# Fourier mixing and low-rank mixer: prologue reordered around the arrival of x, filter mirrors cut in pieces, group 0 in fixed order, two batches' steps moved and every reload brought forward in the main loop

## The chip, the cores and the metric

The kernel runs on one core of one Trainium2 chip. The metric is device time in microseconds (us). All runs used here are fast. Each kernel has one profiled run; its span is a little shorter than the run's time (596.6 us of span in a run of 598.55 us). Differences of parts are taken from spans and times of day inside a trace, differences between kernels from ratios. A ratio is the mean time of one kernel's fast runs over that of the kernel before in the same rounds, so it is not quite the ratio of the medians quoted beside it.

The engines in the profile are PE (TensorE matmuls), PEld (its weight loads), DVE (VectorE), ACT (ScalarE), POOL (GpSimd) and SP, which issues DMAs. "Half clock" means that the clock records of a trace show TensorE granted 0.5 of its full clock. A "hole" is a time in which PE stands still.

## The reference

```python
# x (8, 3136, 256), filt_r and filt_i (1569, 256)
X = np.fft.rfft(x, axis=1)
y = np.fft.irfft(X * (filt_r + 1j*filt_i), n=3136, axis=1)
# U (3136, 32), V (32, 3136), w_ch1 (256, 1024), w_ch2 (1024, 256)
h = y.transpose(0, 2, 1) @ U @ V
u = y + h.transpose(0, 2, 1)
out = u + np.maximum(u @ w_ch1, 0) @ w_ch2
```

The Fourier transform of length 3136 = 64 x 49 is done as matmuls with constant matrices: stage 1 over 64 points, a turn, stage 2 over 49 points (z), the product with the filter, and the same way back.

## The kernel before

Batch 0 is worked off alone in a prologue, because nothing else is ready. After it a main loop of 49 groups of 8 steps does the two large matmuls of all batches (`phh` = u @ w1, `pc` = h @ w2), and the transforms of batches 1 to 7 are dealt out over the steps as generators. Engines called `te, ve, se, ge, sy` keep the program's order. Instructions on `nc.tensor` and so on may be moved by the scheduler. In the profile the pinned instructions all have one line, L98, the line of the helper.

Names that return in the views, in the order of the work: `pf` is a result of stage 1 in PSUM (the memory that matmuls write to) and `xh` (for U, `eball`) its copy. `pa` is the turn and `at` its copy; "the first turn" is the first `pa`. `pz` is a result of stage 2 and `uv` its product with the filter. `po` is the first step of the way back and `uh` its copy. U's own steps make `aur`, `ga`, `gb` and `aus`, and the matmuls `ph` use them for the low-rank part.

The prologue's loads and its stage 1, cut:

```python
for c in range(3): load_x(u0, c)                       # POOL's queue
for c in range(3): sy.dma_start(wf[:, ...c...], ...)   # constants of stage 1
sy.dma_start(ulf, ...)                                 # U's last rows
sy.dma_start(mats, mats_d)                             # 366 KB
sy.dma_start(wf[0:64, 3072:3136], ...)                 # 8 KB, for the last rows
...
ve.tensor_copy(ul, ulf)
stage1(... un ..., xhu, 32)             # U, stage 1
stage1_last(32, ul, xhu)                # needs the small wf
fill(4, ...)                            # matmuls on junk, to keep PE's clock
aur = u_turn()
se.copy(fab[0:NR, :, 31, :], st31[0:NR])
mirror(2, 0, ge)
for c in range(3):                      # x of batch 0 in three chunks
    for dh in range(2):
        stage1(... u0.x[c] ..., xh[dh], 128)
    if c == 0: gab = u_z(aur)           # ga on ACT, gb on DVE
    if c == 1: u_rows(aur); ph0 = ...   # aus
    if c: fill(4, ...)
... stage1_last for x
mirror(0, 0, ve); turn1(0); mirror(0, 1, ve); turn1(1)
for i in range(16):                     # pairs of frequencies
    ... turn1(i + 2)
    if i == 3: mirror(1, 0, ve); mirror(1, 1, se)    # 12 slots each
    if i == 9: mirror(2, 1, se)                      # 12 slots
    uvs0[i] = z_product(u0, 2*i, at[i], te, ve)      # pz, then uv on DVE
    ... i1_turned(i - 2)                # po, then uh on ACT
    ... h_part at i = 7, 11, 13
```

`mirror` copies the filter `fab` from partitions 0..63 to 64..127.

The main loop's plan, cut. `f1` is stage 1 of a batch and writes its result to DRAM (`ct`). `mid` reads it back in the other order (`a2`, shown as `a<-ct`) and does z and the way back (`pe`). `ranks` is the low-rank part.

```python
def mid(u):
    for c in range(2): a2[c] = load_a2(u, c)
    for k in range(0, NK, 2): ... z_product ...; yield
...
if u.n == 1:
    deal(f1s[1], 7, 2, 9);    deal(mids[1], 17, 13, 37); rank = (38, 40)
elif u.n == 2:
    deal(f1s[2], 7, 26, 38);  deal(mids[2], 17, 43, 75); rank = (s-20, s-18); x_step[14] = u
else:
    deal(f1s[u.n], 7, s-78, s-66); deal(mids[u.n], 17, s-56, s-23)
    rank = (s-20, s-18); x_step[s-92] = u          # s = 48 * u.n
```

## Time and profile before

| | before |
|---|---|
| time, median of 3 runs | 597.58 us (597.38 to 598.76) |
| stage 1 of x starts / first turn | 21.6 / 35.1 us |
| the 16 filter products (uv) | 36.9 to 62.4 us, 25.5 us |
| last uh copy to first phh | 63.6 to 69.2 us |
| main loop, from the first phh | 527.3 us |

The page of the kernel before: PE's busy time, and the span in 40 slices of 14.9 us with busy tenths, the granted clock in tenths, and DMA's busy tenths.

```profile
PE 554.9 (93%) x4803; PEld 397.3 (67%) x4803; DVE 348.3 (58%) x375; ACT 354.2 (59%) x608; POOL 45.6 (8%) x83
...
PE   5678894999999999999999999999999999999996
...
PEclk9588996999999999999999999999999999999998
DMA  9991048335965479365856568546945642432112
```

PE is full from slice 8 to the last. Slices 1 to 5 (prologue) and slice 7 are not, and in slices 2 and 7 the clock is also low. The sum of 93% hides this: most of the time that can be seen to be lost lies in the first 105 us.

The waits of PE before, over the whole span: total in us, times, longest.

```profile
PE pz L325 <- DMA a<-ct: 12.1, 6, 7.9
PE pf L98 <- DMA wf<-wf: 7.8, 2, 6.4
PE po L98 <- ACT uh L98: 5.6, 3, 2.9
PE pur L98 <- DVE gb L98: 1.9, 1, 1.9
...
PE ph L98 <- ACT aus L98: 1.1, 1, 1.1
```

The first line is the main loop; the other four are the prologue. PE in the prologue before, in order of time (start, duration, what, how many, idle time before and what ended it):

```profile
9.73 0.61 PE L98 MATMUL pf<-wf,un 128*32 128x128 f16 x8 [1.39 <-DMA wf<-wf]
16.77 0.21 PE L98 MATMUL pf<-wf,ul 64*32 64x64 f16 x1 [6.44 <-DMA wf<-wf]
16.91 1.89 PE L98 MATMUL fill<-un,junk 128*128 128x512 f16 x4
18.86 2.76 PE L98 MATMUL ptu<-mats,eball 32*98 32x32 f16 x32
21.55 1.89 PE L98 MATMUL pf<-wf,x 128*128 128x128 f16 x16
```

A single small matmul on U's last rows holds PE until 16.8 us, because its 8 KB of constants stand in SP's queue behind 366 KB: by the DMA records the packets of `mats` run from 7.7 to 13.7 us, those of the small wf from 11.2 to 15.3. The trace's semaphores show x's chunks landed at 10.2, 13.2 and 16.9 us, while their stage 1 begins only at 21.6.

The chain of waits before around batch 1's reload (start, duration, what):

```profile
85.04 4.50 DMA ct<-al
...
89.61 10.98 DMA a<-ct
...
100.63 0.58 PE pz L325
```

PE runs out of earlier work at 92.7 us and stands still for 7.9 us.

### The profile page before, as it was taken

The page shows a single profiled execution, that of the slowest core. Times are in us where ns is not written, and L with a number is a line of the kernel's source. Part 1 is how long each engine was busy: PE and PEld are TensorE (multiplying, and loading weights), DVE is VectorE, ACT ScalarE, POOL GpSimd, SP SyncE. Part 2 cuts the span into 40 slices and gives each one's busy share as a digit, 9 for nine tenths or more (in the row PEclk, how much of TensorE's full clock was granted, in tenths as well). Part 3 has the DMA queues.
Part 4 walks back from the last instruction along what each step waited for, and adds up shares of the span by engine and source line. Part 5 has one row for each costly group of instructions (what it writes and reads, how often), then busy time and mean ns, then how long its engine had stood idle before and what let it go on. Part 6 is the DMA issues. An engine that isn't in the chain of part 4 may idle for free.

```text
span 596.6 us, 11873 instructions
## 1 busy us (share of the span) xinstructions
PE 554.9 (93%) x4803; PEld 397.3 (67%) x4803; DVE 348.3 (58%) x375; ACT 354.2 (59%) x608; POOL 45.6 (8%) x83
## 2 busy tenths in 40 slices
PE   5678894999999999999999999999999999999996
PEld 2445572667767767776777667776777677777775
DVE  4366651896586476656674476547665566433331
ACT  1367662476667556665666566665666566666562
POOL 6650010000100001000100010000100000000000
PEclk9588996999999999999999999999999999999998
DMA  9991048335965479365856568546945642432112
GB/s 203 138 168 27 2 129 203 127 113 180 229 198 151 151 211 205 133 188 174 180 170 192 176 156 197 167 150 187 202 139 181 169 145 75 141 107 89 55 52 106
DMA packets 68610, 88.97 MB, mean 149 GB/s; under 512 B 5644, under 2 KB 52734, under 8 KB 68556
## 3 DMA queue, kind: packets, MB, share of 16 engines
q1 hardware_dynamic: 61516, 72.41, 38.7%
q0 software_dynamic: 7040, 15.82, 16.3%
q8 instruction: 37, 0.61, 0.4%
q14 instruction: 17, 0.14, 0.1%
HBM read 55.85 MB, written 48.17 MB: 174 GB/s over the span
## 4 chain that ended last, share of the span: by engine, by line
PE 78%; DMA 9%; ACT 7%; DVE 3%; issue 2%; SPq 1%; ACTq 0%
PE pc L625 25%; PE phh L602 24%; PE pe L450 7%; DMA a<-ct 6%; PE pz L325 5%; PE pc L630 3%; PE pu L585 3%; PE pf L419 2%; ACT asb L422 2%; DMA wf<-wf 2%; ACT e L461 1%; ACT h L604 1%; PE ph L554 1%; PE po L98 1%; ACT fab L98 1%
## 5 line engine op out<-in xcount | busy, mean ns | idle before, releaser
L604 ACT ACTIVATE h<-phh 128x512 f16<-128x512 f32 x392 | 233.6, 598 | 126.8 <-PE phh L602 125.6
L625 PE MATMUL pc<-w2sb,h 128*128 128x256 f16 x1568 | 241.1, 273 | 0.1
L602 PE MATMUL phh<-ut,w1sb 128*128 128x512 f16 x784 | 239.5, 382 | 0.6 <-DVE ut L594 0.3
L625 PEld LDWEIGHTS <-h 128*128 128x128 f16 x1568 | 150.4, 98 | 77.3 <-issue 2.5
L336 DVE TENSOR_TENSOR uv<-pz,fab 113x1024 f16<-113x1024 f32 x112 | 135.4, 1219 | 36.8 <-PE pz L325 35.9
L636 DVE COPY och<-pc 128x512 f32<-128x512 f32 x98 | 67.6, 690 | 123.2 <-PE pc L630 122.2
L602 PEld LDWEIGHTS <-w1sb 128*128 128x128 f16 x784 | 96.4, 145 | 18.3 <-issue 3.3
L461 ACT CAST e<-pe 98x512 f16<-98x512 f32 x112 | 65.0, 587 | 52.0 <-PE pe L450 51.6
L594 DVE CAST ut<-pu 128x1024 f16<-128x1024 f32 x48 | 58.7, 1222 | 21.2 <-PE pu L585 21.2
L450 PE MATMUL pe<-uv,mats 113*98 113x512 f16 x210 | 62.5, 378 | 0.0
L630 PE MATMUL pc<-mats,ut 128*128 128x128 f16 x392 | 54.1, 220 | 0.0
L325 PE MATMUL pz<-a,mats 98*128 98x512 f16 x105 | 39.5, 385 | 13.0 <-DMA a<-ct 12.1
L630 PEld LDWEIGHTS <-ut 128*128 128x128 f16 x392 | 38.4, 98 | 6.2 <-issue 0.2
L585 PEld LDWEIGHTS <-eball 96*128 96x128 f16 x768 | 29.1, 98 | 9.9 <-issue 1.9
L450 PEld LDWEIGHTS <-mats 113*98 113x98 f16 x210 | 25.4, 124 | 12.6 <-issue 2.8
L488 DVE COPY eball<-h 32x2048 f16<-32x2048 f16 x34 | 22.1, 680 | 19.7 <-ACT h L515 18.4
L425 DVE CAST asb<-pf 128x1024 f16<-128x1024 f32 x21 | 25.6, 1221 | 13.2 <-PE pf L419 13.1
L585 PE MATMUL pu<-sv,eball 96*128 96x64 f16 x768 | 30.6, 193 | 0.5
L160 POOL COPY x<-h 1x1 f16<-1x1 f16 x18 | 2.5, 178 | 363.6 <-ACT h L604 363.6
L419 PE MATMUL pf<-x,wf 128*128 128x256 f16 x168 | 26.1, 273 | 0.6
L98 DVE TENSOR_TENSOR uv<-pz,fab 113x1024 f16<-113x1024 f32 x16 | 19.0, 1221 | 5.8 <-PE pz L98 4.0
L422 ACT CAST asb<-pf 128x1024 f16<-128x1024 f32 x21 | 21.3, 1015 | 1.1 <-PE pf L419 1.0
(88 smaller groups left out, 282.6 us busy)
## 6 DMA issues: line engine op xcount, KB each, us to landing
out_dram<-och SPq DMA_DIRECT2D x48, 512.0 KB
x<-in_x_dram POOLq DMA_DIRECT2D x24, 512.0 KB, 8.5
a<-ct SPq DMA_DIRECT2D x28, 392.0 KB
ct<-e SPq DMA_DIRECT2D x56, 196.0 KB
ct<-asb SPq DMA_DIRECT2D x21, 512.0 KB
eball<-ct SPq DMA_DIRECT2D x84, 128.0 KB
wf<-wf SPq DMA_DIRECT2D x3, 256.0 KB
w1sb<-in_moe_w_ch_dram POOLq DMA_DIRECT2D x1, 512.0 KB, 5.3
```

The source lines that it names most:

```text
L325: te.matmul(pz, wz[0], a2, start=True, stop=True)
L336: ve.tensor_mul(uv.rearrange("p f k d -> p f (k d)"), zin, fin)
L419: nc.tensor.matmul(pf[:, j], wf[:, 128 * (8 * c + r):128 * (8 * c + r) + 128], u.x[c][:, r, :], start=True, stop=True, skip_group_check=True)
L450: nc.tensor.matmul(pe[0:98, :, :], gz[0][f], uv[:, f, :, :], start=(f == 0), stop=(f == 1))
L461: nc.scalar.copy(e[:, i:i + 2, :], pe[0:98, :, :])
L585: nc.tensor.matmul(pu[:, dh, 64 * i:64 * i + 64], e2[:, s, 128 * dh:128 * dh + 128], sv[:, 64 * r:64 * r + 64], start=(i == 0), stop=True, ...
L594: nc.vector.tensor_copy(dst, src)
L602: nc.tensor.matmul(ph, w1v[:, dh, :, t], gr.ut[:, dh, :], start=(dh == 0), stop=(dh == 1))
L604: nc.scalar.activation(h, ph, RELU)
L625: nc.tensor.matmul(o, gr.h[tt][:, i * 128:(i + 1) * 128], w2sb[:, tt * DM:(tt + 1) * DM], start=(tt == 0), stop=False, skip_group_check=True)
L630: nc.tensor.matmul(o[:, dh * 128:dh * 128 + 128], gr.ut[:, dh, i * 128:i * 128 + 128], idn, start=False, stop=(dh == 1), skip_group_check= ...
L636: nc.vector.tensor_copy(gr.och[:, 2 * y:2 * y + 2, :], gr.pc.rearrange("p (j d) -> p j d", j=2))
```

## The change

Its intent: start on x when x is there; put U's later steps between the chunks of x; cut the mirrors into pieces so that no engine is blocked long; fix the order in group 0; and give batch 1's and batch 2's steps better places. The diff, cut to its core (left out, among smaller things: in the prologue stage 1 now turns over four PSUM buffers in place of six, because the third pair is left to the fills):

```diff
+    sy.dma_start(wf[0:64, 3072:3136], wf_d[0:64, 3072:3136])
     sy.dma_start(ulf, ...)
-    sy.dma_start(mats, mats_d)
-    sy.dma_start(wf[0:64, 3072:3136], wf_d[0:64, 3072:3136])
+    se.dma_start(mats, mats_d)
...
-    fill(4, ...)
-    aur = u_turn()
+    fill(6, ...)
...
-    mirror(2, 0, ge)
+    mirror(20, 26, 0, ge); mirror(20, 26, 1, ge)
+    (the two sv guards and sv loads, moved here)
+    mirror(26, NK, 0, ge); mirror(26, NK, 1, ge)
     for c in range(3):
         ... stage1 of x chunk c
+        if c < 2: fill(6, ...)
-        if c == 0: gab = u_z(aur)
-        if c == 1: u_rows(aur); ...
-        if c: fill(4, ...)
+        if c == 0: aur = u_turn()
+        if c == 1: gab = u_z(aur)
...
-        if i == 3: mirror(1, 0, ve); mirror(1, 1, se)
-        if i == 9: mirror(2, 1, se)
+        if i in (2, 4, 6):                    # four slots each
+            a = 2 * i + 4
+            mirror(a, a + 4, 0, ve); mirror(a, a + 4, 1, se)
+        if i in (9, 10): u_rows(aur, i - 9)   # aus, in halves
...
     def mid(u): ... a2[c] = load_a2(u, c)
+        yield
...
(group 0: turn2 and stage4 on te, ve, se; DVE and ACT swapped in turn2; h rows in halves of a tile)
...
+    f, m, z, q, xs = {1: (2, 15, 39, 40, None), 2: (38, 54, 80, 82, 26)}.get(
+        u.n, (s - 78, s - 56, s - 23, s - 20, s - 92))
+    deal(f1s[u.n], 7, f, f + (7 if u.n == 1 else 12))
+    plan[m - 5].append(mids[u.n])             # the reload, five steps ahead
+    deal(mids[u.n], 17, m, z)
```

More of the change, by code (lines that the diff above doesn't have):

```diff
@@ L221, in load_filters, with mirror @@
                 dram(src.tensor, (63 - a) * DM, [[64 * DM, 24], [-DM, n], [1, DM]]))
-    def mirror(i, f, eng):
-        a, z = PARTS[i], PARTS[i + 1]
+    def mirror(a, z, f, eng):
         dst, src = fab[64:128, f, a:z, :], fab[0:64, f, a:z, :]
@@ L239 @@
     for i in range(2):
-        ge.tensor_copy(sv[64 * i:64 * i + 1, 0:1], vnat[0][32:33, 0:1])
-        sy.dma_start(sv[64 * i:64 * i + 32, :], sv_d[32 * i:32 * i + 32, :])
-    for i in range(2):
         ge.tensor_copy(
@@ L251, with fill @@
     xhu = bass.AP(tensor=eball.tensor, offset=eball.offset, ap=[[eball.ap[0][0], 32], [98, NK], [1, 98]])
-    fill_to = ps.tile([128, 512], F32, tag="w", bufs=1, name="fill")
-    def fill(n, dst, rhs):
+    fill_to = ps.tile([128, 512], F32, tag="o", bufs=2, name="fill")
+    def fill(n, rhs):
         for _ in range(n):
-            te.matmul(dst, junk[:, 0:128], rhs, start=True, stop=True, skip_group_check=True)
-    fill(16, fill_to, junk)
+            te.matmul(fill_to, junk[:, 0:128], rhs, start=True, stop=True, skip_group_check=True)
+    fill(16, junk)
     banks = [0]
@@ L264, in stage1 @@
         for p0 in range(0, len(chunks), 4):
-            pf = ps.tile([128, 16, NK], F32, tag=("z", "m", "o")[banks[0] % 3], bufs=2, name="pf0")
+            pf = ps.tile([128, 16, NK], F32, tag=("z", "m")[banks[0] % 2], bufs=2, name="pf0")
             for j in range(4):
@@ L278, in stage1_last @@
     def stage1_last(m, cols, dst):
-        pf = ps.tile([128, 2, NK], F32, tag=("z", "m", "o")[banks[0] % 3], bufs=2, name="pf0")
+        pf = ps.tile([128, 2, NK], F32, tag=("z", "m")[banks[0] % 2], bufs=2, name="pf0")
         banks[0] += 1
@@ L301, in u_z, with u_rows @@
         return ga, gb
-    def u_rows(aur):
-        pt = ps.tile([128, 2, 512], F32, tag="w", bufs=1, name="pur")
-        for h in range(2):
-            te.matmul(pt[0:98, h, :], mats[0:98, 648:746], aur[:, 16 * h:16 * h + 16, :],
-                      start=True, stop=True)
-        se.copy(aus.rearrange("p (h k) c -> p h (k c)", h=2), pt[0:98])
+    def u_rows(aur, h):
+        pt = ps.tile([128, 512], F32, tag="z", bufs=2, name="pur")
+        te.matmul(pt[0:98], mats[0:98, 648:746], aur[:, 16 * h:16 * h + 16, :], start=True, stop=True)
+        se.copy(aus[:, 16 * h:16 * h + 16].rearrange("p k c -> p (k c)"), pt[0:98])
     at, uvs0, po = {}, {}, {}
@@ L368 @@
     stage1_last(32, ul, xhu)
-    fill(4, fill_to, un.rearrange("p r c -> p (r c)")[:, 0:512])
-    aur = u_turn()
+    fill(6, un.rearrange("p r c -> p (r c)")[:, 0:512])
     u0.xl = sb.tile([64, DM], F16, tag="xl", bufs=2, name="xl")
@@ L373 @@
     se.copy(fab[0:NR, :, 31, :], st31[0:NR])
-    mirror(2, 0, ge)
+    mirror(20, 26, 0, ge)
+    mirror(20, 26, 1, ge)
+    for i in range(2):
+        ge.tensor_copy(sv[64 * i:64 * i + 1, 0:1], fab[0:1, 0, 20, 0:1])
+        sy.dma_start(sv[64 * i:64 * i + 32, :], sv_d[32 * i:32 * i + 32, :])
+    mirror(26, NK, 0, ge)
+    mirror(26, NK, 1, ge)
     for c in range(3):
@@ L377 @@
             stage1([(8 * c + r, u0.x[c][:, r, 128 * dh:128 * dh + 128]) for r in range(8)], 128, xh[dh], 128)
+        if c < 2:
+            fill(6, u0.x[c][:, 0:2, :])
         if c == 0:
+            aur = u_turn()
+        if c == 1:
             gab = u_z(aur)
-        if c == 1:
-            u_rows(aur)
-            ph0 = ps.tile([128, 2, 512], F32, tag="w", bufs=1, name="ph0")
-        if c:
-            fill(4, ph0[:, 1], u0.x[c][:, 0:2, :])
     for dh in range(2):
         stage1_last(128, u0.xl[:, 128 * dh:128 * dh + 128], xh[dh])
-    mirror(0, 0, ve)
+    ph0 = ps.tile([128, 2, 512], F32, tag="w", bufs=1, name="ph0")
     turn1(0)
-    mirror(0, 1, ve)
     turn1(1)
+    mirror(0, 8, 0, ve)
+    mirror(0, 8, 1, ve)
     for i in range(NK // 2):
@@ L393 @@
             turn1(i + 2)
-        if i == 3:
-            mirror(1, 0, ve)
-            mirror(1, 1, se)
-        if i == 9:
-            mirror(2, 1, se)
+        if i in (2, 4, 6):
+            a = 2 * i + 4
+            mirror(a, a + 4, 0, ve)
+            mirror(a, a + 4, 1, se)
         uvs0[i] = z_product(u0, 2 * i, at[i], te, ve)
@@ L401 @@
             i1_turned(i - 2)
+        if i in (9, 10):
+            u_rows(aur, i - 9)
         if i in (7, 11):
@@ L406 @@
     i1_turned(14)
-    h_part(ph0, gab, (12, 13, 14))
+    h_part(ph0, gab, range(12, 16))
     i1_turned(15)
-    h_part(ph0, gab, (15,))
     def f1(u):
@@ L507, in h_rows @@
         hp = sb.tile([128, DM], F16, tag="hp", bufs=1, name="hp")
-        nc.scalar.activation(hp, ph, COPY, scale=1.0 / 32.0)
+        (nc.scalar if u.n else se).activation(hp, ph, COPY, scale=1.0 / 32.0)
         return hp
@@ L512, in h_sum, with turn2 @@
         pk = ps.tile([128, 512], F32, tag="z", bufs=2, name="pk")
-        nc.tensor.matmul(pk[0:64, 0:DM], kr, hp, start=True, stop=True)
+        (nc.tensor if u.n else te).matmul(pk[0:64, 0:DM], kr, hp, start=True, stop=True)
         u.h1 = sb.tile([64, DM], F16, tag="h1", bufs=2, name="h1")
-        nc.scalar.copy(u.h1[32:64, :], pk[32:64, 0:DM])
-    def turn2(u, g):
+        (nc.scalar if u.n else se).copy(u.h1[32:64, :], pk[32:64, 0:DM])
+    def turn2(u, g, te=nc.tensor, ve=nc.vector, se=nc.scalar):
         if g < 6:
@@ L532, in turn2 @@
                     b = 4 * (4 * g + j) + s
-                    nc.tensor.matmul(pt[0:96, s, 128 * dh:128 * dh + 128],
-                                     uh[:, dh, b:b + 3].rearrange("p b k -> p (b k)"), idn,
-                                     start=True, stop=True, skip_group_check=True)
+                    te.matmul(pt[0:96, s, 128 * dh:128 * dh + 128],
+                              uh[:, dh, b:b + 3].rearrange("p b k -> p (b k)"), idn,
+                              start=True, stop=True, skip_group_check=True)
             dst = t[:, 2 * j:2 * j + 2, :] if g < 6 else t[:, u.n:u.n + 1, :]
             if j % 2:
-                nc.scalar.copy(dst, pt[0:96, 0:m])
+                ve.tensor_copy(dst, pt[0:96, 0:m])
             else:
-                nc.vector.tensor_copy(dst, pt[0:96, 0:m])
-            if j == 3:
-                put_h(u, t[32:64], 8)
-            elif g == 6:
-                put_h(u, e2l[32:64, u.n:u.n + 1, :], 1)
+                se.copy(dst, pt[0:96, 0:m])
+            if g == 6:
+                put_h(u, e2l[32:64, u.n:u.n + 1, :], 1, ve)
+            elif j % 2:
+                put_h(u, t[32:64, 2 * j - 2:2 * j + 2], 4, ve)
             yield
@@ L577, in stage4 @@
         gr.ut = sb.tile([128, 2, 512], F16, tag="ut", bufs=3, name="ut")
+        first = gr is groups[0]
         for dh in range(2):
-            for i in range(8):
+            for i in (0, 2, 4, 6, 1, 3, 5, 7) if first else range(8):
                 if gr.last:
@@ L584, in stage4 @@
                     r, e2 = 8 * gr.g + s, u.e2[gr.g]
-                nc.tensor.matmul(pu[:, dh, 64 * i:64 * i + 64], e2[:, s, 128 * dh:128 * dh + 128],
-                                 sv[:, 64 * r:64 * r + 64],
-                                 start=(i == 0), stop=True, skip_group_check=True)
+                (te if first else nc.tensor).matmul(
+                    pu[:, dh, 64 * i:64 * i + 64], e2[:, s, 128 * dh:128 * dh + 128],
+                    sv[:, 64 * r:64 * r + 64], start=(i == 0), stop=True, skip_group_check=True)
         dst = gr.ut.rearrange("p h (c q s) -> p h c q s", q=64, s=2)
         src = pu.rearrange("p h (c s q) -> p h c q s", q=64, s=2)
-        if gr is groups[0]:
-            nc.vector.tensor_copy(dst[:, 0], src[:, 0])
-            nc.scalar.copy(dst[:, 1], src[:, 1])
+        if first:
+            ve.tensor_copy(dst[:, 0], src[:, 0])
+            se.copy(dst[:, 1], src[:, 1])
         else:
@@ L647 @@
     h_sum(u0, h_rows(u0, ph0[:, 0, 0:DM]))
-    for _ in turn2(u0, 0):
+    for _ in turn2(u0, 0, te, ve, se):
         pass
@@ L665 @@
         s = 48 * u.n
-        if u.n == 1:
-            deal(f1s[1], 7, 2, 9)
-            deal(mids[1], 17, 13, 37)
-            rank = (38, 40)
-        elif u.n == 2:
-            deal(f1s[2], 7, 26, 38)
-            deal(mids[2], 17, 43, 75)
-            rank = (s - 20, s - 18)
-            x_step[14] = u
-        else:
-            deal(f1s[u.n], 7, s - 78, s - 66)
-            deal(mids[u.n], 17, s - 56, s - 23)
-            rank = (s - 20, s - 18)
-            x_step[s - 92] = u
+        f, m, z, q, xs = {1: (2, 15, 39, 40, None), 2: (38, 54, 80, 82, 26)}.get(
[3 more added lines that the diff above has]
+        deal(mids[u.n], 17, m, z)
+        rank = (q, q + 2)
+        if xs is not None:
+            x_step[xs] = u
         for w in rank:
```

## The prediction

> **What bounds the kernel.** The page shows PE busy 93% of 596.6 us, but in two regimes. In the timeline the prologue lasts until the first phh matmul at 69.2 us and is latency-bound; after it TensorE runs nearly without holes for 527 us. In the view of waits (PE) the holes after 69 us are "pz <- DMA a<-ct": 12.1 us, one of 7.9 (93 to 101 us), several of about 1.2. The clock records then show half clock at 95 to 105 us, about 2 us more. In the prologue PE waits 7.8 us on the wf DMAs (6.4 us on the small one, landed at 16.6 us behind mats), 5.6 us for uh copies on ACT behind two mirrors of 2.75 us, 3.0 us for gb and aus.
>
> **What the change does.**
> 1. mats leaves SP's queue and the small wf goes first: U's last step can run near 11.5 us, not 16.8. x landed at 10.2, 13.2 and 16.9 us, yet its stage 1 started at 21.6; now near 14, with U's turn and z between chunks. More fills (18 for 8, 0.22 to 0.43 us each) should hold the clock. The Trainium skill, "TensorE: Matmul & The Clock Gate" (What's actually happening), says that the clock halves after an idle window of about 3.4 us; the trace agrees: half clock at 13.1 to 33.6 us, from a hole at 10.3 to 16.8. Limit: gb (2 x 1.23 us, DVE) precedes the last evacuations. I expect turn1 at 27 to 30 us (35.1 before).
> 2. Filters landed at 21.1, 27.4, 32.7 us, early enough. But DVE's first two mirrors can meet POOL's two 3.52 us sv copies (24 to 31 us). "SBUF — State Buffer" (SBUF: two separate sides) says DVE and POOL take turns on a shared port pair; before, one mirror took 0.89 us while POOL was copying, its twin 0.69. So the first uv near 31 us (36.9 before), gain 6.
> 3. Mirrors in thirds: 0.92 us on ACT, 0.35 on DVE (estimates, a third of 2.75 and 0.95), one less on ACT; two aus copies (about 0.55) move in. The phase of 16 uv products took 25.5 us; DVE alone needs 16 x 1.22 plus 1.1. I expect 22 to 23, gain 3.
> 4. Group 0 pinned, engines swapped, halves of put_h: from last uh to first phh 5.9 us before, about 4.4 after.
> Loop start about 58.7 us, gain 10.5.
> 5. Batch 1's mid two steps later, its a2 loads three steps earlier and ahead of the store, batch 2's x 12 steps later. Before, a2 was issued at 89.6 us, behind x loads and a store, and landed at 100.6, 11 us. Later a2 loads took 4.6 to 5.8. I expect a hole under 2 us, no half clock: gain 8 to 9.
> 6. Every batch loads a2 five steps ahead: the 1.2 us holes go, gain 3 to 4. Batch 2's mid is denser (DVE nearly full): minus 1.
>
> **Critical path.** All of it: PE's order is serial. Sum about -21 us.
>
> **Prediction: 576 us**, 568 to 586 with 80%. Faster by over 2%: 0.89; within 2%: 0.10; slower: 0.01.
>
> **What would show it.** First x matmul at 13 to 15 us; turn1 at 27 to 30; uv phase 22 to 23 us; first phh at 57 to 61; no half clock from 35 us to the end; PE's wait for a<-ct under 3 us in all; loop 514 to 518 us.
>
> **What would make it wrong.** PE cold to 30 us, so turn1 comes at 32; DVE mirrors blocked by POOL for over 4 us; mats on ACT's queue delaying wf, un or x0; POOL's mirrors late for product 10; batch 1's reload late for group 6; batch 2's dense stretch stalling.

## The result, and the profile after

| | before | after |
|---|---|---|
| time, median of 4 runs | 598.17 us (597.38 to 600.17) | 573.53 us (572.27 to 574.66) |
| ratio | | 0.9583 (0.955 to 0.9615) |
| stage 1 of x starts / first turn | 21.6 / 35.1 us | 14.7 / 26.5 us |
| first to last uv | 36.9 to 62.4, 25.5 us | 29.5 to 51.3, 21.8 us |
| last uh to first phh | 5.64 us | 5.64 us |
| first phh | 69.2 us | 58.3 us |
| main loop | 527.3 us | 512.1 us |

The change is faster by 4.2%, inside the predicted range. By the profiled spans 10.9 us come from the prologue and 15.3 us from the loop, together 26.2 us.

The same lines of the page after (a slice is 14.3 us):

```profile
PE 546.6 (96%) x4809; PEld 394.5 (69%) x4809; DVE 349.4 (61%) x382; ACT 351.6 (62%) x611; POOL 48.3 (8%) x86
...
PE   6788989999999999999999999999999999999996
...
PEclk9879999999999999999999999999999999999999
DMA  9992154857956585755945685656756533331112
```

The hole in slice 7 is gone, and PE is fuller in the prologue. The waits of PE after:

```profile
PE pf L98 <- DVE eball L98: 3.6, 1, 3.6
PE pf L98 <- DVE xh L98: 2.6, 1, 2.6
PE pz L319 <- DMA a<-ct: 2.2, 1, 2.2
...
PE po L98 <- ACT uh L98: 0.4, 1, 0.4
```

The waits for wf are gone and the wait for the reload has shrunk from 12.1 to 2.2 us. But two waits for DVE are new. The prologue after, on PE:

```profile
11.27 0.76 PE L98 MATMUL pf<-wf,un 128*32 128x128 f16 x8 [3.60 <-DVE eball L98]
11.97 0.23 PE L98 MATMUL pf<-wf,ul 64*32 64x64 f16 x1
12.13 2.74 PE L98 MATMUL fill<-un,junk 128*128 128x512 f16 x6
14.66 1.22 PE L98 MATMUL pf<-wf,x 128*128 128x128 f16 x16
...
17.11 1.63 PE L98 MATMUL ptu<-mats,eball 32*98 32x32 f16 x32
```

U's last row is done at 12.2 us, not 17. And DVE after, over the same stretch and up to the first product:

```profile
10.46 0.17 DVE L98 CAST ul<-ulf 64x32 f16<-64x32 f32 x1 [3.33 <-DMA ulf<-in_moe_U_dram]
10.55 2.00 DVE L98 CAST eball<-pf 32x512 f16<-32x512 f32 x4
...
22.56 2.46 DVE L98 TENSOR_SCALAR gb<-pzu 64x1024 f16<-64x1024 f32 x2 [1.94 <-ACT ga L98]
25.05 1.55 DVE L98 CAST xh<-pf 128x512 f16<-128x512 f32 x4
26.64 2.74 DVE L98 COPY fab<-fab 64x2048 f16<-64x2048 f16 x2
29.48 2.36 DVE L98 TENSOR_TENSOR uv<-pz,fab 113x1024 f16<-113x1024 f32 x2
```

Three things can be read here. DVE's first job is a copy whose data land at 10.4 us, and U's copies stand behind it: this is PE's new wait of 3.6 us. (Before, the same copy waited to 10.96 us and PE went on, because six PSUM buffers took all of U's stage 1; with four, PE must wait until one is emptied. No run separates the two causes.) gb stands ahead of x's last copies: PE's wait of 2.6 us. And two mirrors take 2.74 us, singly 2.07 and 0.74. The first of them began while POOL ran its second copy (24.63 to 28.15 us), the second did not start until 28.63:

```profile
21.15 7.01 POOL L98 COPY sv<-vnat 32x1568 f16<-32x1568 f16 x2
28.11 0.78 POOL L98 DMA_DIRECT2D w1sb<-in_moe_w_ch_dram  x1
```

A fourth is on ACT, where a copy of the 31st row of the filter waits for its data, with x's first copies on ACT behind it:

```profile
16.95 0.62 ACT L98 CAST fab<-st 49x512 f16<-49x512 f32 x1 [4.30 <-DMA st<-in_filt_i_dram]
```

The long mirror agrees with the Trainium skill, "SBUF — State Buffer" (SBUF: two separate sides), which says of the port pair shared by DVE and POOL that the loser "fully blocks".

The chain of waits after, at batch 1's reload:

```profile
74.49 4.40 DMA ct<-al
...
78.96 4.54 DMA a<-ct
...
83.54 0.38 PE pz L319
```

The reload itself now takes 4.54 us in place of 10.98.

### The profile page after: what moved, and what is told of

Its sections match the earlier page's. It is cut to its first block, busy times and chain, and to the rows that moved or that the text cites. A ratio compares the mean times of both kernels' runs of the same rounds, so it can differ in the third digit from the quotient of the medians.

```text
span 570.4 us, 11903 instructions
## 1 busy us (share of the span) xinstructions
PE 546.6 (96%) x4809; PEld 394.5 (69%) x4809; DVE 349.4 (61%) x382; ACT 351.6 (62%) x611; POOL 48.3 (8%) x86
## 4 chain that ended last, share of the span: by engine, by line
PE 83%; ACT 5%; DMA 2%; DVE 1%; issue 1%; ACTq 0%; SPq 0%
PE pc L626 28%; PE phh L603 28%; PE pe L449 8%; PE pz L319 4%; PE pu L586 4%; PE pc L631 4%; PE pf L418 3%; ACT asb L421 2%; PE ph L554 1%; ACT e L460 1%; ACT h L605 1%; PE pt L533 1%; DMA a<-ct 1%; DMA ct<-al 1%; DVE uv L330 1%
## 5 line engine op out<-in xcount | busy, mean ns | idle before, releaser
L330 DVE TENSOR_TENSOR uv<-pz,fab 113x1024 f16<-113x1024 f32 x112 | 135.6, 1219 | 33.4 <-PE pz L319 32.8
L603 PEld LDWEIGHTS <-w1sb 128*128 128x128 f16 x784 | 97.4, 145 | 20.3 <-issue 3.2
L586 PEld LDWEIGHTS <-eball 96*128 96x128 f16 x752 | 28.7, 98 | 10.1 <-issue 1.9
L449 PEld LDWEIGHTS <-mats 113*98 113x98 f16 x210 | 25.5, 124 | 10.3 <-issue 1.1
L488 DVE COPY eball<-h 32x2048 f16<-32x2048 f16 (+1 forms) x38 | 22.0, 610 | 16.0 <-ACT h L515 15.4
L586 PE MATMUL pu<-sv,eball 96*128 96x64 f16 x752 | 30.5, 193 | 0.4
L418 PEld LDWEIGHTS <-wf 128*128 128x128 f16 x168 | 15.3, 97 | 9.0 <-ACT asb L421 2.2
```

The lines of the kernel that those rows point to most:

```text
L330: ve.tensor_mul(uv.rearrange("p f k d -> p f (k d)"), zin, fin)
L418: nc.tensor.matmul(pf[:, j], wf[:, 128 * (8 * c + r):128 * (8 * c + r) + 128], u.x[c][:, r, :], start=True, stop=True, skip_group_check=True)
L449: nc.tensor.matmul(pe[0:98, :, :], gz[0][f], uv[:, f, :, :], start=(f == 0), stop=(f == 1))
L586: (te if first else nc.tensor).matmul(pu[:, dh, 64 * i:64 * i + 64], e2[:, s, 128 * dh:128 * dh + 128], sv[:, 64 * r:64 * r + 64], start=( ...
L603: nc.tensor.matmul(ph, w1v[:, dh, :, t], gr.ut[:, dh, :], start=(dh == 0), stop=(dh == 1))
```

## The experiments

Twelve kernels ran, each in 3 rounds beside the kernel before, and all gave correct results. Ratios are to the kernel before; the whole change has 0.9583.

### e1: only the loop's plan

The edit is the kernel before with the new plan and the new `yield` in `mid`, and nothing else.

> The kernel before, with only the new places of batch 1's, 2's and the later batches' steps in the main loop (and the early reload). If prologue and loop gain separately, the first phh stays at 69.2 us, PE's wait for a<-ct falls from 12.1 to under 3 us, no half clock comes at 95 to 105 us, and the time falls by about 15 us, ratio near 0.975. Rival: the loop's gain needs the earlier start or the reordered group 0 (they share the scheduler's order), then it is under 8 us, ratio above 0.987.

Measured: 581.45 us, ratio 0.9719 (0.9684 to 0.9754). PE's hole at batch 1 is 2.0 us and is the only wait of over 0.2 us in the loop. The loop takes 513.5 us; half clock did come once, at 93.4 to 96.8 us.

### e2: only the prologue

The edit is the changed kernel with the old plan and without the `yield`.

> The changed kernel with the loop's plan as before. Separate gains: first phh at 58.3 us, the a<-ct wait of about 8 us and the half clock after it come back, time about 11 us below before, ratio near 0.982, and the two gains of e1 and e2 add up to the 25 us of the whole change. Rival: an earlier loop start only lengthens the wait for a2 (the data do not come earlier), then the ratio is above 0.99.

Measured: 588.43 us, ratio 0.9844 (0.9805 to 0.9883). The first phh comes at 58.4 us, the reload's hole is 7.5 us and the loop takes 528.5 us. The two parts add up: 0.0281 + 0.0156 = 0.0437, against 0.0417 for the whole change, within the intervals. Starting the loop earlier does not lengthen the hole, because everything from stage 1 of batch 1 onward moves with it.

### e3: group 0 as before

```diff
-    for _ in turn2(u0, 0, te, ve, se):
+    for _ in turn2(u0, 0):          # with turn2, h_rows, h_sum, stage4 as before
```

> The changed kernel with group 0 (its turn, its h rows and its last product) as before: free order, old engines, h rows put once per tile. My prediction gave the new form 1.5 us. The trace shows 5.6 us from the last uh copy to the first phh in both kernels, so the theory now is that it gained nothing: ratio 0.958 plus or minus 0.001. If the prediction's step was right the ratio is 0.961.

Measured: 573.78 us, ratio 0.959 (0.956 to 0.962). From the last uh to the first phh there are 5.48 us, against 5.64 with the fixed order. This part of the change bought nothing that these runs can see. The changed kernel's DVE at the end of the prologue suggests why:

```profile
56.22 0.42 DVE L98 COPY eball<-h 32x1024 f16<-32x1024 f16 x1
56.56 0.41 DVE L488 COPY eball<-h 32x1024 f16<-32x1024 f16 x1
57.00 0.69 DVE L538 CAST eball<-pt 96x512 f16<-96x512 f32 x1
57.61 0.68 DVE L98 CAST ut<-pu 128x512 f16<-128x512 f32 x1
```

Lines L488 and L538 belong to group 1, which is not pinned. Pinning orders the pinned instructions among themselves only, and the scheduler put group 1's work ahead of group 0's last copy (`ut`). That this is the cause was not tested.

### e4: mirrors in the old pieces

```diff
-        if i in (2, 4, 6): (four slots, DVE and ACT)
+        if i == 3: mirror(8, 20, 0, ve); mirror(8, 20, 1, se)
+        if i == 9: mirror(20, NK, 1, se)
```

with one mirror of 12 slots on POOL, as before.

> The changed kernel with mirrors in the old large pieces (12 slots, two of them 2.75 us on ACT). Theory: PE waits for uh copies behind them again, the 16 uv products take 25 us in place of 21.8, time 3 us more, ratio near 0.963, half clock returns inside that stretch. Rival: DVE was the limit and the pieces changed nothing but their place: ratio 0.958 to 0.960.

Measured: 579.49 us, ratio 0.9693 (0.9655 to 0.9731), so the pieces are worth 0.011 or 6.6 us (6.0 by the medians), twice what was expected. The 16 products take 28.2 us (21.8 with pieces, 25.5 before the change). PE's longest item, and DVE's waits from 29 to 58 us, in e4:

```profile
PE po L98 <- ACT uh L98: 4.3, 3, 2.2
```

```profile
DVE uv L98 <- PE pz L98: 5.6, 8, 2.0
DVE uv L98 <- ACT fab L98: 2.3, 2, 1.7
```

Two mirrors of 2.75 us on ACT stop PE (4.3 us), directly stop DVE (2.3 us), and half clock returns at 37.1 to 40.6 and 47.4 to 54.2 us. In the changed kernel the same three waits are 0.4, 0.6 and 0 us. Without the pieces the earlier start would have lost 2.7 us again in this phase.

### e5: batch 2's x early again

```diff
-    2: (38, 54, 80, 82, 26)
+    2: (38, 54, 80, 82, 14)
```

> The changed kernel, but batch 2's x (1.5 MB) loaded at step 14 again, not 26. If contention with those loads made the 11 us of batch 1's first reload, the first product's wait grows from 2.25 us to 6 us or more and half clock follows: time up by 5 to 8 us, ratio 0.966 to 0.972. Rival: the two later steps and the place ahead of the store did it, then the wait stays near 2 us and the ratio at 0.958.

Measured: 579.17 us, ratio 0.9699 (0.9681 to 0.9717), 6.9 us above the change by the ratios, 5.6 by the medians. The chain of waits in e5:

```profile
74.54 4.48 DMA ct<-al
79.09 9.23 DMA a<-ct
88.36 0.58 PE pz L319
```

The hole is 7.0 us again, with half clock from 83.5 to 93.7 us. x of batch 2 was issued at 74.9 to 76.5 us and its last part landed at 91.5. The two later steps and the place ahead of the store are still in this kernel; they do not help. So this load made the long reload: 9.2 us here, 11 before, 4.5 without it. That the two compete for the DMA engines fits the records: from 74.5 to 88.5 us the packets of POOL's queue, which has x's loads alone, take 67% of the engines' time and those of SP's queue 30.5%; in the changed kernel POOL's queue moves nothing over that stretch.

### e6: batch 1's products two steps earlier

```diff
-    1: (2, 15, 39, 40, None)
+    1: (2, 13, 37, 38, None)
```

> The changed kernel with batch 1's reload and products two steps earlier, where they were before (x of batch 2 still late). If the two steps are what hides the reload, the wait grows from 2.25 us to about 4.3 us with half clock after it, ratio near 0.961 to 0.963. If they matter little, because the order on PE is set elsewhere, ratio 0.958.

Measured: 573.51 us, ratio 0.9612 (0.959 to 0.9634), at most 0.003 from the whole change; the hole is 1.6 us, not longer. The place in the plan is a wish; the order that PE gets is the scheduler's. The traces fit this. From the issue of the last write (`ct<-al`) to batch 1's first product, subtract the hole, and what is left is the work that PE had in between:

| kernel | write to first product | hole | PE's work between |
|---|---|---|---|
| before | 15.59 us | 7.89 | 7.7 |
| after | 9.05 us | 2.25 | 6.8 |
| e1 | 9.51 us | 2.01 | 7.5 |
| e2 | 15.24 us | 7.51 | 7.7 |
| e5 | 13.82 us | 7.02 | 6.8 |
| e6 (step 13) | 9.34 us | 1.61 | 7.7 |
| e9 (step 15) | 9.25 us | 2.45 | 6.8 |
| e10 (step 17) | 9.34 us | 2.77 | 6.6 |

The work between is 6.6 to 7.7 us, whatever step the plan names. The hole follows the length of the reload chain, and that falls to about 9 us (8.4 to 10.1) in every kernel without the early x load. Nor could the reload start sooner: in each trace it is issued within 0.1 us after the last store of batch 1 (`ct<-al`) has landed, at 79.0 us in the changed kernel and, without any lead, in e7 too.

### e7: no lead for the reload

```diff
     for c in range(2): a2[c] = load_a2(u, c)
-    yield
...
-    plan[m - 5].append(mids[u.n])
```

> The changed kernel without the five steps between a batch's reload and its first product: both at the same step. Theory: the waits of about 1.2 us of batches 4 to 6 come back and batch 1's grows by some us, ratio 0.966 or more; each steady batch takes 64.6 us again in place of 62.86. Rival: the steady gain of 1.75 us a batch came from elsewhere, then steady batches stay at 62.9 us.

Measured: 579.68 us, ratio 0.971 (0.9692 to 0.9728), 7.6 us above the change by the ratios, 6.2 by the medians; the loop takes 519.7 us, against 512.1. PE's wait for the reload in e7:

```profile
PE pz L319 <- DMA a<-ct: 5.3, 4, 2.1
```

Batch 1's hole is 2.1 us as with the lead (so here the guess failed); the other three are 1.3, 0.5 and 1.4 us, in three of the later batches. Three of the four steady batches (48 steps of phh) take 63.9 to 64.8 us in place of 62.86. The waits explain 3.1 of the 7.6 us. Half clock after batch 1's hole (84.9 to 88.3 us) adds about 1.7 us, an estimate: 12 matmul starts took 3.4 us there, which is halved at full clock. That half clock is no sure effect of the missing lead: the hole before it is no longer than with the lead (2.1 and 2.25 us). Some 3 us, spread thinly, stay unexplained.

### e8: a version meant to be better

The waits of the changed kernel name what to move.

```diff
-    ve.tensor_copy(ul, ulf)                 # ahead of U's copies
     stage1(U); fill(6)
-    se.copy(fab[0:NR, :, 31, :], st31[0:NR])
     for c in range(3):
         stage1 of x chunk c
+        if c == 0: ve.tensor_copy(ul, ulf); stage1_last(U); fill(3); u_turn
-        if c == 1: gab = u_z(aur)
+        if c == 1: fill(6); pz = ...         # the matmuls of z alone
     stage1_last(x)
+    se.copy(fab[0:NR, :, 31, :], st31[0:NR])
+    (POOL: sv copies, after its mirrors)
+    ga on ACT, gb on DVE
```

> A version meant to beat the changed kernel, from its trace: DVE waits 3.3 us for U's last row and holds up U's copies and PE (3.6 us); ACT waits 4.3 us for the 31st filter row; gb (2.46 us, DVE) stands before the last copies of x; a mirror waits 1.4 us for POOL's sv copy. Here U's last row comes after x's first chunk, the filter row and ga, gb after the last copies of x, the sv copies last on POOL. Expected: turn1 at 18 to 20 us (26.5), first uv at 21 to 23 us (29.5), first phh at 50 to 52 us (58.3), no half clock between 15 us and the end of the uv phase, time 566 plus or minus 2 us, ratio 0.946. Rival: filters (landed 25.9 and 28.1 us) then hold the products back and the gain is under 3 us.

Measured: 568.43 us, ratio 0.9515 (0.9497 to 0.9533). The first turn comes at 20.3 us (26.5), the first uv at 24.3, the first phh at 53.3: about 2 us later than hoped, 5 us earlier than the change. The filters did not hold it back (the products take 22.0 us). Two expectations failed: the time is above 566 plus or minus 2 us, and half clock came at 26.5 to 29.9 us. Several copies moved at once here, and no run tells which of them gave the first turn its 6.2 us. PE in e8:

```profile
10.51 1.06 PE L98 MATMUL pf<-wf,x 128*128 128x128 f16 x16
12.48 0.20 PE L98 MATMUL pf<-wf,ul 64*32 64x64 f16 x1 [0.91 <-DVE ul L98]
...
17.13 0.60 PE L98 MATMUL pzu<-aur,mats 98*128 98x512 f16 x3
```

The wait of 3.6 us has gone and x's first chunk starts 4.2 us earlier.

### e9: gb made on POOL

```diff
-    ve.tensor_scalar_mul(gb[0:64], pz[64:128], 1.0 / 49)
-    ve.tensor_scalar_mul(gb[64:128], pz[0:64], -1.0 / 49)
+    ge.tensor_copy(gb[0:64], ga[64:128])
+    ge.tensor_scalar_mul(gb[64:128], ga[0:64], -1.0)
```

To give gb its place, POOL's mirrors also stand after it in the program.

> e8 with gb made on POOL from ga (two copies of 64x1024, exact) in place of 2.46 us on DVE ahead of the first mirror. If DVE's gb is what held the first uv at 24.3 us, it comes at about 22 us, first phh at 51 us, time 566 us, ratio near 0.948. Rival: filters (second part landed 25.9 us in the changed kernel) hold the third pair's mirror and products, and the uv phase grows by what the start gains: ratio 0.951.

Measured: 567.19 us, ratio 0.9474 (0.944 to 0.9508). The first uv comes at 22.9 us, 1.4 earlier, but the products take 22.9 us, 0.9 more: DVE's mirrors meet POOL's copies (the three pieces take 0.96, 0.76 and 1.06 us; in e8, where only the second began during one, 0.42, 0.99 and 0.48, together 0.89 us less). The first phh comes at 52.9 us, only 0.5 earlier than in e8, and the intervals of e8 and e9 touch.

### e10: e9 with batch 1's products at step 17

```diff
-    1: (2, 15, 39, 40, None)
+    1: (2, 17, 41, 41, None)
```

> e9 with batch 1's products two steps later still (17). If more distance hides the reload, the hole of 1.6 to 2.2 us at batch 1's first product goes: 1 to 2 us less than e9. If the reload for group 6 is then late, a new wait before that group's product of equal size or more appears.

Measured: 567.30 us (565.44 to 572.13), ratio 0.9468 (0.9428 to 0.9507). Nothing is gained. The table above shows why: PE's work between did not grow. Neither expected outcome came true. The profiled run, the slowest of the four, has a hole of 2.8 us; the ratio fits the other three runs alone (all four give 0.949).

### e11: no fills

The edit is without the 15 fill matmuls between U, the chunks and z. The text calls this e8 without fills; the kernel that ran was built on e9, so it is to be held against e9.

> e8 without its 15 fills between U, x chunks and z (about 3.7 us of PE). If fills earn their place by the clock, half clock returns before turn1 and the uv phase or its start is slower: time 1 to 4 us above e8. If not, turn1 comes 1 to 2 us earlier and the time is equal or lower.

Measured: 566.05 us, ratio 0.9461 (0.9429 to 0.9493), equal to e9 within the intervals. Half clock at 12.7 to 19.5 and 22.9 to 26.3 us did no harm to the time; the first turn is at 20.9 us (21.1 in e9).

### e12: the changed kernel without fills

```diff
-    fill(6, un...)
...
-        if c < 2: fill(6, u0.x[c]...)
```

> The changed kernel without its 18 fills (5.7 us of PE in its trace). My prediction had the fills hold the clock; its trace has half clock at 11.6 to 15.0 and 25.2 to 35.5 us in spite of them. If they earn their place, turn1 (26.5 us) or the first uv (29.5) comes later without them, and the time rises by 1 to 4 us. If DVE's gb and ACT's wait for the filter row set that time, turn1 stays within 1 us and the ratio at 0.958.

Measured: 573.03 us, ratio 0.9573 (0.955 to 0.9596). The first turn comes at 26.0 us (26.5 with fills), the first uv at 29.6 (29.5). PE is at half clock from 17.2 to 34.2 us, its second and third chunks of x take 1.87 us in place of about 1.06, and nothing is lost: PE in e12 waits for ACT and DVE instead of filling. The wait for ACT lies behind the late copy of the filter's row (4.8 us of waiting on ACT here). x's stage 1 starts at 11.8 us here and at 13.0 in e2, and the first turn comes at 26.0 us in both; so its start alone does not set that time.

```profile
18.25 1.87 PE L98 MATMUL pf<-wf,x 128*128 128x128 f16 x16 [3.57 <-ACT xh L98]
...
25.29 0.21 PE L98 MATMUL pf<-wf,xl 64*128 64x64 f16 x1 [2.46 <-DVE xh L98]
```

## Why the prediction was right, point by point

The time was predicted as 576 us (568 to 586) and measured as 573.5. The signs and most sizes held; two steps failed and two were mis-sized.

1. **Stage 1 of x near 14 us, the first turn at 27 to 30.** Measured: 14.7 and 26.5 us. The reason given (the small wf behind mats) was right: PE's 7.8 us of waits for wf went to none. That PE would then wait 3.6 us for DVE (U's last rows, and two PSUM buffers fewer) was missed; e8 takes the wait away. It cost little: with x's stage 1 starting 1.7 us sooner (e2) and 2.9 us sooner (e12), the first turn came 0.5 us sooner. The step "more fills should hold the clock" failed: half clock came at 25.2 to 35.5 us in spite of them, and e12 without any has the same time. The clock had no price there that e12 can see: PE was waiting for gb and for copies.
2. **First uv near 31 us, with DVE and POOL meeting.** Measured: 29.5 us, and one mirror blocked (2.07 us against 0.74). The gain was 7.4 us, predicted 6.
3. **Mirrors in pieces, 22 to 23 us for the products, gain 3.** Measured: 21.8 us, gain 3.7. But their worth is larger than that term says: with the earlier start and the old pieces the phase would have taken 28.2 us (e4), so that 6.6 us hang on them. The estimate compared with the old phase and not with the old pieces in the new place.
4. **Group 0 in fixed order: 4.4 us in place of 5.9.** This step failed: the stretch is 5.64 us in both traces (5.90 in both, counted from ACT's last uh copy as the prediction did), and e3 shows no gain. Pinned work was still interleaved with unpinned work, which may be why.
5. **Batch 1: a hole under 2 us, gain 8 to 9.** The hole is 2.25 us, a little over, and there is no half clock after it, so the size held. The second half of that is partly luck: holes of 2.01 to 2.77 us at the same place had half clock after them in e1, e3, e7, e9 and e10, and holes of 1.61 to 2.51 us had none in e4, e6, e8, e11 and e12. Of the three reasons that the prediction named together, only one works: batch 2's x no longer loads beside the reload (e5: 7.0 us of hole without that). The loads "three steps earlier" could not start sooner than the landing of the store, and e7's hole without them is 2.1 us. The two later steps do nothing measurable (e6, e10), and the place ahead of the store did not help where x was early (e5).
6. **The lead of five steps, gain 3 to 4, and 1 us lost in batch 2.** Mis-sized: e7 gives the lead 7.6 us, or some 6 without the half clock that may be chance. A steady batch went from 64.6 to 62.9 us, 1.7 us, where the waits counted had been 1.2; of the rest 0.3 us lies in the phh matmuls, whose times from start to next start sum to 21.5 us a batch in place of 21.85. Batch 2's denser stretch could not be singled out: its 48 steps take 67.3 us for 65.3, but work crosses the batches' borders.

The prologue was predicted to gain 10.5 us and gained 10.9. The loop was predicted at 514 to 518 us and took 512.1. Summing PE's gaps of over 0.2 us in the loop gives 13.0 us before and 2.8 after, and 20 matmul starts at half clock, 4.6 us, are gone, which is worth about half of that. The remaining 3 us or so are in small differences that no experiment here names.

The best kernels are e9, e10 and e11, at 0.946 to 0.947 (566 to 567 us), which the runs do not tell apart. e11 is the simplest of the three.

## What to carry to other kernels

Find what a reload competes with before giving it more distance: here moving another batch's load by 12 steps cut the hole from 7.0 to 2.25 us (e5), while moving the consumer by two steps changed nothing that could be measured, since the order on PE did not follow the plan. Cut long copies on an engine whose next job feeds the critical chain, and value such a cut together with the earlier start it protects. After moving work forward, look at the first wait of each in-order engine: a copy waiting for late data at the head of DVE's or ACT's queue stops all that is ready behind it, and fills on PE did not repair that here.

## What the Trainium skill lacked or had wrong

- "TensorE: Matmul & The Clock Gate" (What's actually happening) gives half clock after an idle window and full clock after a busy one, with free-running windows of about 3.4 us. The records agree in their steps (3.4, 6.8, 10.2 us), but the page does not say how idle a window must be. A hole of 2.10 us was followed by half clock for 3.4 us (e7), a hole of 2.25 us at the same place by none (the changed kernel), and three holes of 0.69, 2.55 and 0.52 us within 4.2 us (22.4 to 26.5 us) went with 10.2 us of half clock from 25.2 us on. The length of a hole does not decide it: 2.01 us was followed by half clock in e1, 2.51 us by none in e4.
- The same page advises keeping PE warm. It does not say that this is worth nothing where PE is not what the chain waits for, as in the prologue here: without fills, chunks of x took 1.87 us in place of 1.06 and the kernel's time was 573.03 us against 573.53.
- "SBUF — State Buffer" was right about the shared port pair, for small copies as for large ones, and the runs add how a block ends. In all 24 cases in which a mirror on DVE began during a copy on POOL, over the traces of all kernels, it ended 0.55 to 0.56 us (8 slots, 0.69 alone) or 0.28 us (4 slots, 0.42 alone) after POOL's copy, however early it had begun. In e9, e10 and e11 a piece that began during POOL's multiply for gb ended 1.47 us before it did; why stays open.
- "DMA: Bandwidth & Descriptors" (Issuing engines are not separate DMA queues) says that issuing from several engines only saves the sequencer's issue time. Here mats went to ACT's queue and an 8 KB load came ahead of it in SP's, and PE's waits for wf fell from 7.8 us to none. No run separates the two moves. But the DMA records show more than issue time: `mats` was issued 2.1 us earlier (0.74 us, not 2.80), and its packets were through 9.7 us earlier (4.0 us, not 13.7), no longer standing behind the wf loads of SP's queue.
